# Real and imaginary halves of a spectrum stacked on the 128 partitions, in a kernel of two long convolutions mixed by a gate

## The chip, the cores and the metric

The kernel runs on one core of one Trainium2 chip. The metric is the device time of one execution in microseconds (us). The time of the kernel before is 413.97 us, the median of 3 runs (412.12 to 418.88).

## The reference, cut to what matters

Two sequences of 2048 positions with 448 channels are convolved along the positions, each with a kernel of its own per channel, and mixed by a gate. Both convolutions are written as products of spectra of padded length 4096.

```python
g = sigmoid((u * gate_w).sum(-1, keepdims=True))
# branch A: the kernel comes from 256 complex modes per channel
K  = einsum("dn,dnl,dn->dl", C, exp(dt * A * l), dt * B).real
a  = irfft(rfft(pad(u)) * rfft(pad(K)))[:2048] + u * Dskip
# branch B: the kernel ssm_k is an input; its signal is made from k and v
kv = shift_conv4(k, shift_k) * v
b  = u * (irfft(rfft(pad(kv)) * rfft(pad(ssm_k)))[:2048] + kv * ssm_D)
out = g * a + (1 - g) * b
```

## The kernel before, in words

**Layout.** A position is 64 a + b (a from 0 to 31, b from 0 to 63). A tile in natural order has 4 groups of channels times 32 values of a on its 128 partitions, and the 64 values of b times 112 channels along its free axis. The 112 channels are two halves h of 56, and these are worked on in four quarters H of 14 (`NW`), so one quarter holds 4 x 2 x 14 channels.

**One transform** of a quarter takes two steps. `spread` (L209) is the transform over a: for each of 14 channel columns one TensorE matmul takes the data (b and h, 128 columns) as weights and the table `W` (256 columns) as the moving operand. The result has b and h on the partitions, and 32 rows k, real and imaginary, along the free axis. ScalarE copies it from PSUM to the tile `zs` (L216, through `evac` at L534). `transform` (L219) is the transform over b, with the twiddle factors in its tables: for each of the 32 rows k it runs four matmuls of 56 columns (L229 to L232), cosine and sine against the real and the imaginary half, added up in PSUM. Each table is zero where h of the row and of the column differ, so half of the array multiplies by zero. ScalarE copies back to `zs` in pieces of 448 columns, two for every eight rows.

**Product and inverse.** `products` (L265) multiplies two spectra X and K in four VectorE products of 1792 columns, into T0 and in place. `stage_a` (L238) is the first step of the inverse: 14 columns with four matmuls of 256 columns each, 56 in all, added up in PSUM, copied to `U` by ScalarE. `stage_b` (L252) is the second step, 128 matmuls of 28 columns, and VectorE reads its PSUM in the epilogues (L682 for branch B, L688 and L691 for A).

**The kernel of branch A** is generated in eight blocks, two for a quarter (`KGen.block`, L294). VectorE builds powers by a doubling scheme (L311, L312, L316, L325, L332), 448 small matmuls with their weights (L345, `pk`) sum over the modes, a gather (L386, `ps_g`) rounds positions to their place, and the block's part of the quarter is spread (L674). Only then can the quarter's spectrum KA be transformed.

**Order.** `seq` (L747) is B0, B1, A0, B2, A1, B3, A2, A3. `step` (L705) does the inverse of one entry and the forward transforms of the next, and then one block of the kernel generator; behind it come block 7, the transform of KA for quarter 3 in four pieces whose PSUM copies are shared by ScalarE and VectorE (`evac_two`, L536), the products and the last inverse. Every engine works in its own order, which a scheduler writes from priorities when the program is built. Ahead of the loop lie the tables, the generator's setup (`kgen_setup`, L394, whose tables go out to DRAM and come back per block), the first two spectra of branch B, and the gate (L736 to L745: a product on VectorE, 112 matmuls, a sigmoid, two more VectorE passes).

**The kernel of branch B** is loaded by `load_sk` (L606) with eight DMAs that GpSimd issues. `sk_cols` (L613) has ScalarE reorder it into a second buffer `sk` (L616), and VectorE add the skip term to position 0 (L618). SBUF buffers come from rings: tag `q` (5 buffers of 7168 bytes per partition) and tag `hq` (7 of 3584 bytes). PSUM has three buffers of two banks for all matmuls but the generator's.

## Time and profile before

| what | value |
|---|---|
| time, median of 3 runs | 413.97 us |
| time of the profiled execution | 411.89 us |
| its span, first to last instruction | 409.7 us |
| mean granted TensorE clock | 0.845 |
| TensorE busy (matmuls) | 266.6 us, 65% |
| VectorE busy | 298.6 us, 73% |
| ScalarE busy | 225.8 us, 55% |
| GpSimd busy | 38.8 us, 9% |

The profile is one execution, recorded by the hardware. PE is TensorE's matmuls, PEld its weight loads, DVE is VectorE, ACT is ScalarE, POOL is GpSimd, SP is SyncE, which issues most DMAs. A row of the timeline has the start in us from the span's start, the duration, engine, line, operation, out<-in, shapes and a count; in brackets stands the idle time of the engine before it and what ended that. A group of instructions shows the total busy time and the mean duration in ns of one instruction. Durations of neighbours overlap a little, so the distance from start to start is the price of one in a row of many. A window lists the busy time of each engine in a stretch of the span, and the TensorE clock that was granted there, as a share of full speed.

### The profile page before, as it was taken

The numbers are of one execution on the slowest core, as the hardware profiler recorded it, in microseconds if no ns is written. First come the engines' busy times: TensorE is split into PE (matmuls) and PEld (weight loads), VectorE is DVE, ScalarE is ACT, GpSimd is POOL, SyncE is SP. The second block draws the span as 40 slices with busy tenths as digits, with TensorE's granted clock in tenths as the row PEclk, the third lists the DMA queues.
The fourth block names the chain that finished last, engine by engine and source line by source line (L and its number), as shares of the span: only waits on it lengthen the run. The fifth ranks groups of instructions, "written<-read, shape, count | busy, mean of one in ns | idle before, by whom it ended". The sixth has DMA issues, their size and how long they took to land.

```text
span 409.7 us, 13770 instructions
## 1 busy us (share of the span) xinstructions
PE 266.6 (65%) x6224; PEld 231.7 (57%) x6224; DVE 298.6 (73%) x525; ACT 225.8 (55%) x314; POOL 38.8 (9%) x166
## 2 busy tenths in 40 slices
PE   3001694250408997869777787896797997895770
PEld 2001531020408886767767675886597797695660
DVE  7969999755258598997999899899998820422630
ACT  6993948991630473555376266444782654656130
POOL 7940000000540000021000000000000000000000
PEclk9999966866665598996999896996999698898695
DMA  8979904799910012132120212121020000000019
GB/s 164 162 120 184 231 5 135 223 318 210 230 37 13 0 49 89 52 102 80 52 86 2 87 53 86 52 89 48 3 87 6 2 3 5 2 3 2 2 28 153
DMA packets 55826, 33.33 MB, mean 81 GB/s; under 512 B 37016, under 2 KB 53208, under 8 KB 55768
## 3 DMA queue, kind: packets, MB, share of 16 engines
q1 hardware_dynamic: 50200, 29.56, 31.3%
q0 software_dynamic: 1344, 1.98, 2.3%
q10 hardware_dynamic: 4224, 0.92, 1.4%
q8 instruction: 48, 0.79, 0.8%
q14 instruction: 10, 0.08, 0.1%
HBM read 19.84 MB, written 12.62 MB: 79 GB/s over the span
## 4 chain that ended last, share of the span: by engine, by line
PE 36%; DVE 31%; DMA 10%; issue 9%; ACT 8%; POOL 3%; DVEq 0%; ACTq 0%; POOLq 0%; SPq 0%
PE ps_a L247 10%; PE pk L345 7%; DVE kg_P L311 5%; PE ps_b L259 4%; DVE kvt L647 4%; ACT zsK L534 3%; PE ps_gate L739 3%; DMA skraw<-in_B_ssm_k_dram 3%; DMA ed<-ks_r 3%; PE ps_c L215 3%; PE ps L229 2%; DVE ks_ph L435 2%; PE ps L230 2%; PE ps L232 2%; PE ps L231 2%
## 5 line engine op out<-in xcount | busy, mean ns | idle before, releaser
L230 PEld LDWEIGHTS <-s_S 128*128 128x128 bf16 x512 | 52.8, 103 | 21.4 <-issue 21.4
L229 PE MATMUL ps<-zs,s_C 128*128 128x56 bf16 x384 | 46.6, 195 | 14.8 <-ACT zs L534 14.8
L229 PEld LDWEIGHTS <-s_C 128*128 128x128 bf16 x512 | 53.0, 103 | 0.3
L231 PEld LDWEIGHTS <-s_N 128*128 128x128 bf16 x512 | 52.8, 103 | 0.1
L232 PEld LDWEIGHTS <-s_C 128*128 128x128 bf16 x512 | 52.8, 103 | 0.0
L247 PE MATMUL ps_a<-sa_r,zs 128*128 128x256 bf16 x280 | 51.7, 292 | 0.7 <-DVE zs L274 0.4
L534 ACT CAST U<-ps_a 128x1024 bf16<-128x1024 f32 (+1 forms) x32 | 28.4, 908 | 37.0 <-PE ps_a L247 37.0
L534 ACT CAST zs<-ps 128x448 bf16<-128x448 f32 x96 | 43.4, 572 | 6.3 <-PE ps L232 6.3
L230 PE MATMUL ps<-zs,s_S 128*128 128x56 bf16 x384 | 46.6, 195 | 0.0
L231 PE MATMUL ps<-zs,s_N 128*128 128x56 bf16 x384 | 46.6, 195 | 0.0
L232 PE MATMUL ps<-zs,s_C 128*128 128x56 bf16 x384 | 46.5, 195 | 0.0
L311 DVE TENSOR_TENSOR kg_P<-kg_TQ,kg_EQ 128x896 bf16<-128x896 bf16 (+1 forms) x64 | 44.8, 711 | 1.6
L345 PE MATMUL pk<-kg_TP,kg_TQ 128*21 128x32 bf16 x1792 | 30.3, 238 | 21.5 <-issue 16.9
L534 ACT CAST zs<-ps_c 128x1024 bf16<-128x1024 f32 (+1 forms) x48 | 40.2, 957 | 5.6 <-PE ps_c L215 5.6
L345 PEld LDWEIGHTS <-kg_TQ 128*21 128x21 bf16 x1792 | 28.2, 121 | 24.1 <-issue 23.4
L247 PEld LDWEIGHTS <-zs 128*128 128x128 bf16 x280 | 35.6, 143 | 5.0 <-DVE zs L274 1.7
L247 PE MATMUL ps_a<-sa_r,T 128*128 128x256 bf16 x112 | 32.0, 289 | 6.1 <-ACT zs L534 3.1
L311 DVE TENSOR_TENSOR kg_P<-kg_TP,kg_EP 128x896 bf16<-128x896 bf16 (+2 forms) x24 | 29.9, 1246 | 0.7
L312 DVE TENSOR_TENSOR kg_TQ<-kg_P 128x224 bf16<-128x224 bf16 (+2 forms) x64 | 28.8, 450 | 2.1
L651 PE MATMUL ps_v<-kvt,ident 128*128 128x448 bf16 x64 | 19.8, 467 | 14.7 <-ACT kvt L534 7.9
L610 POOL DMA_DIRECT2D skraw<-in_B_ssm_k_dram x32 | 20.6, 651 | 72.5 <-ACT sk L616 68.5
L259 PE MATMUL ps_b<-U,sb_G 128*128 128x28 bf16 x1024 | 26.9, 174 | 0.7 <-ACT U L534 0.7
(162 smaller groups left out, 623.1 us busy)
## 6 DMA issues: line engine op xcount, KB each, us to landing
kg_EP<-ed SPq DMA_DIRECT2D x8, 840.0 KB, 4.2
ed<-ks_E SPq DMA_DIRECT2D x9, 672.0 KB, 4.0
kg_EQ<-ed SPq DMA_DIRECT2D x8, 476.0 KB, 3.4
ed<-ks_r SPq DMA_DIRECT2D x4, 896.0 KB, 9.8
kt<-in_B_k_dram SPq DMA_DIRECT2D x4, 448.0 KB, 9.7
skraw<-in_B_ssm_k_dram POOLq DMA_DIRECT2D x32, 56.0 KB, 3.8
vt<-in_B_v_dram SPq DMA_DIRECT2D x4, 448.0 KB, 8.3
uu<-in_A_u_dram SPq DMA_DIRECT2D x4, 448.0 KB, 11.2
```

The source lines that it names most:

```text
L229: nc.tensor.matmul(re, lhsT=c, rhs=zs[:, 0, k], start=True, stop=False)
L230: nc.tensor.matmul(re, lhsT=s, rhs=zs[:, 1, k], start=False, stop=True)
L231: nc.tensor.matmul(im, lhsT=m, rhs=zs[:, 0, k], start=True, stop=False)
L232: nc.tensor.matmul(im, lhsT=c, rhs=zs[:, 1, k], start=False, stop=True)
L247: nc.tensor.matmul(pt[:, i, :], lhsT=lhsT, rhs=r, start=(n == 0), stop=(n == 3))
L259: nc.tensor.matmul(o, lhsT=G[:, b, r].rearrange("p g a -> p (g a)"), rhs=U[:, r, b].rearrange("p w h -> p (w h)"), start=(r == 0), stop=(r ...
L311: V.tensor_tensor(out=P4[:, i * m:(i + 1) * m].rearrange("p n v c m -> p n v (c m)"), in0=in0, in1=in1, op=ALU.mult)
L312: V.tensor_tensor(out=T[:, dst:dst + n].rearrange("p n v m -> p (n v) m"), in0=P4[:, 0:n].rearrange("p n v c m -> p (n v) c m")[:, :, 0], ...
L345: nc.tensor.matmul(pt[32 * g:32 * g + NQ, hw, :].rearrange("p (i j) -> p i j", i=2), lhsT=TQ[:, :, c, m], rhs=rhs, start=(hf == 0 and c == 0),
L534: nc.scalar.copy(dst, src)
L610: nc.gpsimd.dma_start(raw[g * 32:(g + 1) * 32, :, h, :], sk_src[g, h][:, H * NW:(H + 1) * NW, :])
L651: nc.tensor.matmul(pt[:, i, 0:448], lhsT=ident[:], rhs=t[:, n, 4 * i:4 * i + 4, :].rearrange("p b l -> p (b l)"), start=(n == 0), stop=(n ...
```

## The change

**Stacked halves.** A `zs` tile now has real and imaginary on the two halves of the partitions (64 values of b each), and both halves h of the channels along the free axis: 32 rows k of 112 columns. `spread` does 28 columns with two matmuls each, real and imaginary, each with 64 weight columns and 128 moving columns, placed in the left or the right half of the array's columns (`tile_position`). The table `W2` holds for each row k the three blocks cosine, sine and cosine again, 64 columns each (with signs by partition), so that one full-array matmul of 112 columns transforms a row, and the same row shifted by one block gives the transform with real and imaginary halves exchanged.

**Swapped kernel spectrum.** For kernels (KB and KA) `transform` now makes both versions, `zs` and `zsS`; signals (XB and XA) have one. `products` is then two products of 3584 columns, and `stage_a` takes two matmuls of 128 columns per column of 28, 56 in all. PSUM copies of `transform` are 896 columns wide: four for a signal, eight for a kernel, where each had eight of 448.

**Beside these.** `sk_cols` leaves out ScalarE's reordering: the loaded tile is used as weights, and the skip term is added by GpSimd. The tables of the second step are written by ScalarE straight into place, without masks. The ring `q` has 6 buffers instead of 5, `hq` 6 instead of 7.

```diff
-NBQ = 5
-NBH = 7
+NBQ = 6
+NBH = 6
...
-def spread(nc, psum, W, zs, cols, w0, n, evac):
...
-            nc.tensor.matmul(pt[:, i, :], lhsT=cols(j + i), rhs=W[:], start=True, stop=True)
-        evac(zw[:, :, w0 + j:w0 + j + m, :], pt[:, 0:m].rearrange("p i (rk g) -> p rk i g", g=4))
+def spread(nc, psum, W, zs, cols, groups, evac):
+    for whs in groups:
+        pt = psum.tile([P, 8, 128], f32, name="ps_c", tag="ps")
+        for i, wh in enumerate(whs):
+            x = cols(wh)
+            for r in range(2):
+                nc.tensor.matmul(pt[64 * r:64 * r + 64, i, :], lhsT=x, rhs=W[:, 128 * r:128 * r + 128], start=True, stop=True,
+                                 tile_position=(0, 64 * r))
+        n = len(whs)
+        evac(zs[:].rearrange("p k (g c) -> p (k g) c", g=4)[:, :, whs[0]:whs[0] + n], pt[:, 0:n].rearrange("p i kg -> p kg i"))
...
-            nc.tensor.matmul(re, lhsT=c, rhs=zs[:, 0, k], start=True, stop=False)
-            nc.tensor.matmul(re, lhsT=s, rhs=zs[:, 1, k], start=False, stop=True)
-            nc.tensor.matmul(im, lhsT=m, rhs=zs[:, 0, k], start=True, stop=False)
-            nc.tensor.matmul(im, lhsT=c, rhs=zs[:, 1, k], start=False, stop=True)
-        for r in range(2):
-            evac(zs[:, r, 8 * kk:8 * kk + 8, :].rearrange("p k (g w) -> p k g w", g=4),
-                 pt[:, r, 0:8 * n].rearrange("p (k w g) -> p k g w", k=8, g=4), r)
+def transform(nc, psum, W, zs, evac, ks=range(4), swap=None):
+    n = 8 * NW
+    for kk in ks:
+        jobs = [(0, zs)] if swap is None else [(1, swap), (0, zs)]
+        done = []
+        for first, dst in jobs:
+            pt = psum.tile([P, 2, 512], f32, name="ps_2", tag="ps")
+            for i in range(8):
+                k = 8 * kk + i
+                nc.tensor.matmul(pt[:, i // 4, (i % 4) * n:(i % 4 + 1) * n],
+                                 lhsT=W[:, k, first:first + 2].rearrange("p r s -> p (r s)"), rhs=zs[:, k], start=True, stop=True)
+            done.append((dst, pt))
+        for i, (dst, pt) in enumerate(done):
+            evac(dst[:, 8 * kk:8 * kk + 8].rearrange("p (i k) c -> p i (k c)", i=2), pt[:, :, 0:4 * n], i)
...
+            for n, t in enumerate(terms):
+                nc.tensor.matmul(pt[:, i, :], lhsT=t[:].rearrange("p k (g c) -> p (k g) c", g=4)[:, :, j + i],
+                                 rhs=R[:, 128 * n:128 * n + 128], start=(n == 0), stop=(n == 1))
...
-    TT(out=fl(T0[:]), in0=x0, in1=y0, op=ALU.mult)
-    TT(out=x0, in0=x0, in1=y1, op=ALU.mult)
-    TT(out=y1, in0=x1, in1=y1, op=ALU.mult)
-    TT(out=x1, in0=x1, in1=y0, op=ALU.mult)
-    return T0[:], K[:, 1], X[:, 0], X[:, 1]
+def products(nc, X, K, S, k0=0, k1=32):
+    fl = lambda t: t[:, k0:k1].rearrange("p k c -> p (k c)")
+    for t in (K, S):
+        nc.vector.tensor_tensor(out=fl(t), in0=fl(t), in1=fl(X), op=ALU.mult)
+    return K, S
...
-        sk = hqt([P, NW, 64, 2], "sk")
-        nc.scalar.copy(sk[:].rearrange("p v b h -> p v h b"), raw[:])
-        s0 = sk[:, :, 0, :]
-        V.tensor_tensor(out=s0, in0=s0, in1=dB[:].rearrange("p (h v) -> p v h", h=2)[:, H * NW:(H + 1) * NW, :], op=ALU.add)
+        s0 = raw[:, :, :, 0]
+        nc.gpsimd.tensor_tensor(out=s0, in0=s0, in1=dB[:].rearrange("p (h v) -> p v h", h=2)[:, H * NW:(H + 1) * NW, :], op=ALU.add)
+        return lambda h, w: raw[:, w, h, :]
...
+    def with_swap(zs, ks=range(4), swap=None, ev=None):
+        swap = swap or qt([P, 32, 8 * NW], "zsS")
+        transform(nc, psum, W2, zs, ev or evac, ks, swap)
+        return zs, swap
```

Three places of the order are named in the prediction. The first is VectorE ahead of the gate, where the first signal of branch B has been transformed. L271 to L274 are the products (`T_1125` is T0), L618 adds the skip term to the kernel of quarter 1, L736 begins the gate. Before:

```order
L271 TENSOR_TENSOR T_1125<-zs 128x1792
L272 TENSOR_TENSOR zs<-zs 128x1792
L618 TENSOR_TENSOR sk<-sk,dB 128x14x2
L273 TENSOR_TENSOR zs<-zs 128x1792
L274 TENSOR_TENSOR zs<-zs 128x1792
L736 TENSOR_TENSOR ug<-uu,gw 128x7168
```

With the change (L255 is the product, L716 begins the gate):

```order
L146 TENSOR_SCALAR sb_G<-sb_v,mgB 128x32x32 x8
L255 TENSOR_TENSOR zs<-zs 128x3584
L255 TENSOR_TENSOR zsS<-zsS,zs 128x3584
L716 TENSOR_TENSOR ug<-uu,gw 128x7168
L297 COPY kg_TQ<-kg_EQ 128x224
```

The add has left VectorE, and nothing stands between the products and the gate.

The second is ScalarE in the setup. `ks_cs` are sines that the generator's tables wait for, `ps_c` and the numbered `ps_` tiles are PSUM of `spread` and `transform` for the first kernel of branch B. Before:

```order
L616 COPY sk<-skraw 128x14x2x64
L641 COPY wt<-wraw 128x448
L438 ACTIVATE ks_cs<-ks_ph 128x1792
L534 CAST zs<-ps_c 128x64x16 x3
L534 CAST zs<-ps_c 128x64x8
L438 ACTIVATE ks_cs<-ks_ph 128x1792 x3
```

With the change:

```order
L623 COPY wt<-wraw 128x448
L515 CAST zs<-ps_c 128x128x8 x3
L515 CAST zs<-ps_c 128x128x4
L515 CAST zsS<-ps_626 128x896
L515 CAST zs<-ps_635 128x896
L515 CAST zsS<-ps_646 128x896
L515 CAST zs<-ps_655 128x896
L515 CAST zsS<-ps_666 128x896
L419 ACTIVATE ks_cs<-ks_ph 128x1792
```

Nine PSUM copies now stand ahead of the first of these sines, and the reordering copy `sk` is gone.

The third is ScalarE at the kernel spectrum of quarter 2 of branch A (`zsK`). Before, its eight copies of 448 columns lay between two spreads:

```order
L534 CAST zsK<-ps_c 128x64x12
L534 CAST zsK<-ps_6333 128x448 x2
L534 CAST zsK<-ps_6368 128x448 x2
L534 CAST zsK<-ps_6403 128x448 x2
L534 CAST zsK<-ps_6438 128x448 x2
L534 CAST zs<-ps_c 128x64x16 x3
```

With the change there are eight copies of 896 columns:

```order
L515 CAST zsK<-ps_c 128x128x7 x2
L515 CAST zsS<-ps_5828 128x896
L515 CAST zsK<-ps_5837 128x896
L515 CAST zsS<-ps_5848 128x896
L515 CAST zsK<-ps_5857 128x896
L515 CAST zsS<-ps_5868 128x896
L515 CAST zsK<-ps_5877 128x896
L515 CAST zsS<-ps_5888 128x896
L515 CAST zsK<-ps_5897 128x896
L515 CAST zs<-ps_c 128x128x8 x3
```

The number of copies stays, their width doubles. On TensorE the last block's matmuls (`pk`) stand in the middle of this transform with the change, and ahead of the spread of `kg_KT` before.

More of the change, by code (lines that the diff above doesn't have):

```diff
@@ L128, in stage_a @@
         ph = self.tmp.tile([P, 4, 64], i32, name="sa_ph")
[L129 removed]
+        for i, off in enumerate((off_col[0][:, 0:1], off_col[1][:, 0:1], HALF, QUARTER)):
             self.phases(ph[:, i, :], j[:], s_col, off)
[L131 to L140 removed]
+        R = self.pool.tile([P, 256], bf16, name="sa_R")
+        nc.scalar.activation(R[:], low16(ph[:].rearrange("p i b -> p (i b)")), ACT.Sin, scale=PHASE)
+        return R
     def stage_b(self, pool, qt, hqt, k_col, mask):
@@ L206, in col_of @@
         return self.sel[:, self.var[key]].rearrange("p a b -> p (a b)")
-def spread(nc, psum, W, zs, cols, w0, n, evac):
-    zw = zs[:].rearrange("p r k (w g) -> p (r k) w g", g=4)
-    for j in range(0, n, 4):
-        m = min(4, n - j)
-        pt = psum.tile([P, 4, 256], f32, name="ps_c", tag="ps")
-        for i in range(m):
-            nc.tensor.matmul(pt[:, i, :], lhsT=cols(j + i), rhs=W[:], start=True, stop=True)
-        evac(zw[:, :, w0 + j:w0 + j + m, :], pt[:, 0:m].rearrange("p i (rk g) -> p rk i g", g=4))
@@ new lines, in stage_a @@
+def stage_a(nc, psum, pool, R, terms, evac):
+    U = pool.tile([P, 2, 64, 2 * NW], bf16, name="U", tag="q")
+    for j in range(0, 2 * NW, 8):
+        m = min(8, 2 * NW - j)
+        pt = psum.tile([P, 8, 128], f32, name="ps_a", tag="ps")
+        for i in range(m):
+            for n, t in enumerate(terms):
+                nc.tensor.matmul(pt[:, i, :], lhsT=t[:].rearrange("p k (g c) -> p (k g) c", g=4)[:, :, j + i],
+                                 rhs=R[:, 128 * n:128 * n + 128], start=(n == 0), stop=(n == 1))
+        evac(U[:, :, :, j:j + m].rearrange("p r b c -> p (r b) c"), pt[:, 0:m].rearrange("p i rb -> p rb i"))
```

127 lines of the change are left out of this document (40 added, 87 removed).

## The prediction

> **What bounds the kernel now.** I read the page's shares first, then windows of the engines, then what VectorE waited for behind the gate, then the timelines at the gate and at the end.
>
> ```profile
> PE 266.6 (65%) x6224; PEld 231.7 (57%) x6224; DVE 298.6 (73%) x525; ACT 225.8 (55%) x314; POOL 38.8 (9%) x166
> ```
>
> ```profile
> 124.00:142.40 18.40, 18.11 (x134) 16.73 (x135) 12.03 (x21) 3.83 (x6) 0.00 (x0) 0.50 0.01 3
> 142.40:318.70 176.30, 140.65 (x4179) 129.76 (x4178) 161.96 (x250) 96.15 (x154) 5.01 (x8) 0.92 0.18 59
> 318.70:400.00 81.30, 66.06 (x1518) 59.44 (x1517) 30.41 (x53) 40.51 (x64) 0.00 (x0) 0.86 0.04 7
> ```
>
> The columns are length, then PE, PEld, DVE, ACT and POOL busy, then TensorE's granted clock. No engine bounds the whole. From 142 to 319 us VectorE is busy 92% of the time and paces the loop, with TensorE at 80% close behind. Behind 319 VectorE has little left and TensorE is busy 81%.
>
> ```profile
> DVE ept L688 <- PE ps_b L259: 21.6, 2, 12.0
> DVE T L271 <- ACT zsK L534: 12.2, 1, 12.2
> DVE ug L682 <- PE ps_b L259: 8.5, 3, 7.6
> DVE kg_TP L325 <- PE pk L345: 8.2, 5, 2.3
> ```
>
> These are VectorE's longest waits from 140 us on. The first three lie in the tail. In the loop it waits mainly for `pk`: 8.2 us, five times.
>
> ```profile
> 325.17 2.02 DVE L332 TENSOR_TENSOR kg_TP<-kg_TP,kg_EP 128x3584 bf16<-128x3584 bf16 x1
> 338.29 1.85 PE L345 MATMUL pk<-kg_TP,kg_TQ 128*21 128x32 bf16 x110 [0.62 <-ACT kg_S L534]
> 340.72 1.96 PE L345 MATMUL pk<-kg_TP,kg_TQ 128*21 128x32 bf16 x114 [0.58 <-issue]
> 349.73 1.09 DVE L271 TENSOR_TENSOR T<-zs,zsK 128x1792 bf16<-128x1792 bf16 x1 [12.17 <-ACT zsK L534]
> 360.58 1.50 ACT L534 CAST U<-ps_a 128x1024 bf16<-128x1024 f32 x2 [0.41 <-PE ps_a L247]
> 377.94 0.53 ACT L538 CAST zsK<-ps 128x448 bf16<-128x448 f32 x1 [1.79 <-PE ps L232]
> 385.71 0.39 DVE L274 TENSOR_TENSOR zs<-zs,zsK 128x448 bf16<-128x448 bf16 x1
> 392.35 1.50 ACT L534 CAST U<-ps_a 128x1024 bf16<-128x1024 f32 x2 [0.62 <-PE ps_a L247]
> ```
>
> VectorE finishes its part of the last block at 327.2, and TensorE takes that block's `pk` up only at 338.3: it is 11.1 us behind. I therefore split the time into what lies ahead of the gate, the loop up to 327.2, and the 82.5 us from there to the end at 409.7.
>
> **Prices.**
>
> ```profile
> 362.34 3.59 ACT L534 CAST zs<-ps 128x448 bf16<-128x448 f32 x8 [0.25 <-PE ps L232]
> 138.80 6.57 ACT L534 CAST zs<-ps_c 128x1024 bf16<-128x1024 f32 x8 [0.63 <-PE ps_c L215]
> L311 DVE TENSOR_TENSOR kg_P<-kg_TP,kg_EP 128x3584 bf16<-128x3584 bf16 x8 | 16.2, 2023 | 0.2
> L312 DVE TENSOR_TENSOR kg_TP<-kg_P 128x1792 bf16<-128x1792 bf16 x8 | 8.7, 1087 | 0.1
> L616 ACT COPY sk<-skraw 128x1792 bf16<-128x1792 bf16 x4 | 9.1, 2276 | 3.9 <-DMA skraw<-in_B_ssm_k_dram 3.9
> 258.37:264.64 6.27, 6.27 (x64) 1.00 0.11 22
> 264.48:267.95 3.47, 3.47 (x137) 1.00 0.33 117
> L247 PEld LDWEIGHTS <-zs 128*128 128x128 bf16 x280 | 35.6, 143 | 5.0 <-DVE zs L274 1.7 <-issue 0.8 <-DVE kg_P L311 0.7
> 310.77 0.77 PE L386 MATMUL ps_g<-kg_S,ga_sel 128*32 128x112 bf16 x52
> ```
>
> The two windows are one `stage_a` and one `transform` on TensorE alone. `stage_a` streams 56 x 256 columns in 6.27 us, 2.29 columns per ns. With half the columns it takes 3.1 us if weight loads stay hidden, and 56 x 0.143 = 8.0 if each load shows in full. In `transform` a load and its matmul come every 26 ns (3.47 us over 137), so loads do overlap; I take 3.3, a saving of 3.0. A signal's `transform` streams 3584 columns, 1.6 us instead of 3.5; a kernel's two streams take 3.1.
>
> A ScalarE cast of 448 columns costs 3.59/8 = 0.45 us from start to start. The eight of the spread are six of 1024 and two of 512 (the row names the first shape only), so a column costs 0.8 ns and a cast of 896 is 0.81. A signal then holds ScalarE 3.2 us instead of 3.6, a kernel 6.5, which is 2.9 more. The copy `sk` (2.28) goes. The spreads cast as many columns as before, and their writes in runs of 8 elements instead of 16 I cost at nothing, since `U` was already written in runs of 8.
>
> A product of 3584 columns costs 2.02, so a pair 4.05 instead of four times 1.09: 0.3 less.
>
> The new `spread` has no row: 64 weight columns, 128 moving ones, half of the array. The gather shows four matmuls in four parts of the array: 52 start within 0.77 us. About 37 of a block's 58 have 112 columns, some 4100 columns in 1.06 us, 1.7 times `stage_a`'s rate, so parts of the array do work at once. At that rate 56 x 128 columns take 1.8 us; one after the other, 56 ns each, 3.1. Both hide behind the 3.3 us in which ScalarE empties a spread. If a load of 143 ns shows each time it is 8.0, which is a rival below. I take nothing.
>
> **Ahead of the gate.**
>
> ```profile
> 103.60 2.40 ACT L534 CAST zs<-ps_c 128x1024 bf16<-128x1024 f32 x3
> 109.16 2.71 ACT L534 CAST zs<-ps 128x448 bf16<-128x448 f32 x6 [0.41 <-PE ps L232]
> 112.67 1.09 DVE L272 TENSOR_TENSOR zs<-zs 128x1792 bf16<-128x1792 bf16 x1
> 115.74 2.18 ACT L616 COPY sk<-skraw 128x1792 bf16<-128x1792 bf16 x1 [3.87 <-DMA skraw<-in_B_ssm_k_dram]
> 117.95 0.19 DVE L618 TENSOR_TENSOR sk<-sk,dB 128x28 bf16<-128x28 bf16 x1 [4.19 <-ACT sk L616]
> 120.26 3.88 DVE L736 TENSOR_TENSOR ug<-uu,gw 128x7168 bf16<-128x7168 bf16 x1
> 37.57 1.70 ACT L438 ACTIVATE ks_cs<-ks_ph 128x1792 bf16<-128x1792 int16 x1 [6.17 <-DVE ks_ph L435]
> 24.20 4.05 DMA skraw<-in_B_ssm_k_dram
> 37.73 1.27 DVE L137 TENSOR_SCALAR sa_r<-sa_v,mhA 128x128 bf16<-128x128 bf16 x6
> L451 DVE TENSOR_TENSOR ks_E<-ks_cs,ks_mag 128x1792 bf16<-128x1792 bf16 x9 | 9.8, 1083 | 3.7 <-ACT ks_cs L438 3.7
> ```
>
> VectorE's add for a later quarter stands between the products and waits for a DMA and a copy, so two products and the gate come 4.19 us late. With the add on GpSimd, the casts of the spread end near 106.4, four casts behind a cold TensorE near 110.3, two products at 114.4, the gate's product at 118.3 instead of 124.1: -6.0. GpSimd then waits for the DMAs instead; behind it stand only later loads of the same kind, wanted much later. The ring `hq` loses a buffer, but also `sk` and T0; `sb_j` and `sb_v` then share two, which moves the last phases behind eight `sb_G` and is in the 106.4.
>
> Against this, nine casts now stand ahead of the sine at 37.57, for which VectorE's setup waits. The data land at 28.3; the first PSUM tile is there some 2 us later, and the casts take 3.3 + 5 x 0.81 = 7.3. That ends at 37.6, no loss, if TensorE keeps up, and near 40.4, 2.8 late, if it is paced by PSUM buffers that the transposes still hold. I take +1.5. The masks that VectorE no longer applies to the tables gain nothing: it waits for ScalarE right behind the first (3.7 us before `ks_E`), and the second (1.27) filled the wait for the sine at 37.57; the bound is those 1.27. The sum for this part is **-4.5**.
>
> **The loop, up to 327.2.** VectorE stays the pace. Five pairs of products save 1.4 and three adds 0.3. The 8.2 us behind `pk` come from holes in its issue that the change does not touch:
>
> ```profile
> 314.28 2.09 PE L345 MATMUL pk<-kg_TP,kg_TQ 128*21 128x32 bf16 x128 [0.62 <-issue]
> 318.28 0.35 PE L345 MATMUL pk<-kg_TP,kg_TQ 128*21 128x32 bf16 x10 [1.91 <-issue]
> ```
>
> Between none and all of them can go; I take 1.5. So -3.2 (bounds -1.7 and -9.9), and VectorE ends its last block at 327.2 - 4.5 - 3.2 = 319.5. TensorE must be there too: six `stage_a` (18.0) and six signals (11) save 29 us against the 11.1 it was behind. ScalarE gives back 5.5 kernels x 2.9 = 16 and takes 9 off, and was idle 80 of 176 us.
>
> **The tail, from there to the end.** `pk` starts at once: 6.4 with its holes (312.2 to 318.6), then half of the kernel's transform, which now lies behind it, 3.7: products at +10.1, where before they came at +22.5. Products and `stage_a` with its last cast: 4.1 + 4.6 = 8.7, before 12.4. The last signal, `stage_b` and the gather chain to KA's transform: 13.4, before 14.1, of which the last 8.3 stay. The shared transform: VectorE per quarter a cast of 896 (0.62 for 448 before; bounds 0.62 and 1.24, taken 1.1) and two products of about 0.55, 8.6 in all and 1.5 ahead of it, 10.1, before 9.9. The last `stage_a`: 5.6 with TensorE cold at its start, before 7.8. `stage_b`, epilogue, stores: 15.8 as before. Sum 63.7 instead of 82.5: **-18.8**.
>
> Together 319.5 + 63.7 = 383.2 of span, -26.5. The profiled execution has 411.9 with 409.7 of span, so the forecast is 383.2 + 2.2 = 385.4, taken as **386 us**; the profiled execution is 2 below the median of the runs, within their spread.
>
> **The rivals.**
>
> *ScalarE becomes the pace.* A kernel's casts take 6.5 us on a path that ScalarE works in order, between the gather and the next spread; then TensorE is as late for the last `pk` as now, and 11.1 of the tail's gain is lost: 386 + 11 = 397. For it: casts were already slower than `transform`'s matmuls (3.59 against 3.47). Against it: 45% idle in the loop.
> The Trainium skill, "TensorEngine Tiling (Array Packing)", section PSUM Bottleneck, says that after such a gain on TensorE the copies out of PSUM may become the bottleneck. The trace agrees for the single transform, by the two numbers above.
>
> *The waits of VectorE vanish too*: all 8.2 behind `pk` instead of 1.5, 386 - 7 = 379. Against it: the issue holes.
>
> *TensorE turns cold and nothing is gained.* In the window from 124 it was 98% busy and had half the clock, so being busy did not keep it fast. With 141 - 29 = 112 us of work at a clock of 0.92 the loop is TensorE's from a clock of 0.59 down; at 0.5 it takes 206 us, 30 more than 176, of which the gain eats nearly all: about 411, no change. Against it: 0.92 in the loop.
>
> *The half-array spread shows its loads: slower.* 14 spreads lie behind the gate. With one load of 143 ns for each of 56 matmuls a spread takes 8.0 us, 4.7 above ScalarE's 3.3: 66 us, less some 16 that the loop hides: 386 + 50 = 436. It turns slower than now from 6.3 us a spread, 112 ns a matmul. Against it: the gather's 15 ns.
> The same page, under Gotcha 2: Feature Incompatibilities, says that column tiling excludes fast weight load, and the page "TensorE: Matmul & The Clock Gate", section LDWEIGHTS, prices a plain load at its columns over 1.2 per ns; an estimate by it is 53 ns for 64 columns, 3.0 us a spread, which would leave the sum as it is. No row here has such a load.
>
> **How the numbers follow.** Forecast 0.60 (its own range 378 to 394, from the bounds of the setup, the waits and the tail), ScalarE 0.18, no waits 0.07, cold 0.07, slower 0.08. The range from 374 to 403 holds the first three. A measurement of this kernel tells about 2%, 8 us, from no change, so faster is 0.85, same 0.07, slower 0.08.
>
> **What would show it.** Right: `ug` of the gate starts near 116 and no VectorE wait stands between the products; the last `kg_TP` ends near 320 and `pk` follows within 1 us; `stage_a` lasts near 3.3 us on a warm clock; casts of 896 come every 0.8 us; spreads stay at ScalarE's 3.3. Wrong: `pk` of the last block late by over 5 us (ScalarE), a mean clock under 0.7 (cold), over 60 ns a matmul in the spreads (loads), or waits of VectorE in the loop above 15 us.

## The result and the profile after

The changed kernel takes 394.95 us, the median of 4 runs (394.0 to 397.07), where the kernel before took 416.12 on the same chip (4 runs, 412.12 to 418.88). The ratio is 0.953, with a 95% interval from 0.942 to 0.963: faster. On the four other chips used below the kernel before has medians of 412.43 to 413.65 (7 to 19 runs each), so 416.12 is on the high side; against those the gain is 17 to 19 us rather than 21. The forecast of 386 us was 9 too low: inside the range from 374 to 403, which was drawn to hold two rivals as well, but just outside the forecast's own range from 378 to 394. The profiled execution took 395.71 us with a span of 393.9, so against the profile of before (span 409.7) 15.8 us are gone; the forecast was 26.5.

From the page of the changed kernel, the busy shares of the engines and the shares of the chain that ended last; behind it the chain's line from the page of the kernel before.

```profile
PE 250.7 (64%) x5616; PEld 222.4 (56%) x5616; DVE 292.3 (74%) x494; ACT 239.4 (61%) x278; POOL 39.2 (10%) x168
...
PE 30%; ACT 27%; DVE 26%; issue 7%; DMA 6%; POOL 1%; ACTq 0%; DVEq 0%; SPq 0%
```

```profile
PE 36%; DVE 31%; DMA 10%; issue 9%; ACT 8%; POOL 3%; DVEq 0%; ACTq 0%; POOLq 0%; SPq 0%
```

ScalarE's share of the chain went from 8% to 27%, about 33 to 106 us, although its busy time grew by 13.6 us only. It did not become the busiest engine; it came in between, tile by tile, behind TensorE.

The stretches that the prediction used, from the start of the gate's matmuls to VectorE's last block and from there to the end. The columns are length, PE, PEld, DVE, ACT and POOL busy, then TensorE's clock; the kernel after first, then the one before.

```profile
120.80:327.05 206.25, 168.43 (x4328) 156.70 (x4329) 182.83 (x268) 125.58 (x157) 5.66 (x10) 0.86 0.17 51
327.05:393.90 66.85, 41.42 (x971) 39.29 (x968) 20.48 (x31) 30.11 (x37) 0.00 (x0) 0.76 0.17 30
```

```profile
124.29:327.19 202.90, 167.24 (x4365) 153.53 (x4366) 181.94 (x275) 105.95 (x166) 5.01 (x8) 0.87 0.16 52
327.19:409.70 82.51, 57.57 (x1466) 52.37 (x1464) 22.23 (x45) 34.54 (x57) 0.00 (x0) 0.83 0.14 25
```

The gate's matmuls start 3.5 us earlier, the loop behind them is 3.35 us longer, and the tail is 15.7 us shorter. So the whole gain shows behind VectorE's last block, where TensorE and not VectorE had the work.

The waits of VectorE from 139 us on, and the timeline of the tail:

```profile
DVE ept L671 <- PE ps_b L247: 17.1, 2, 8.8
DVE zsS L255 <- ACT zsS L515: 12.1, 3, 9.8
DVE zsK L521 <- PE ps L220: 8.7, 1, 8.7
DVE kg_TP L306 <- PE pk L326: 5.3, 4, 1.6
DVE ug L665 <- PE ps_b L247: 4.2, 4, 1.8
```

```profile
116.78 3.97 DVE L716 TENSOR_TENSOR ug<-uu,gw 128x7168 bf16<-128x7168 bf16 x1
...
318.52 1.16 DVE L665 TENSOR_TENSOR ug<-ps_b,ug 128x448 bf16<-128x448 f32 x2 [1.19 <-PE ps_b L247]
...
325.03 2.02 DVE L313 TENSOR_TENSOR kg_TP<-kg_TP,kg_EP 128x3584 bf16<-128x3584 bf16 x1
329.07 2.46 PE L326 MATMUL pk<-kg_TP,kg_TQ 128*21 128x32 bf16 x150
336.88 2.03 DVE L255 TENSOR_TENSOR zsS<-zsS,zs 128x3584 bf16<-128x3584 bf16 x1 [9.82 <-ACT zsS L515]
342.17 3.53 ACT L515 CAST U<-ps_a 128x1024 bf16<-128x1024 f32 x4 [1.27 <-PE ps_a L234]
353.22 1.86 PE L205 MATMUL ps_c<-WcK,kg_KT 128*64 128x128 bf16 x28 [1.50 <-ACT kg_KT L515]
357.23 1.86 PE L205 MATMUL ps_c<-WcK,kg_KT 128*64 128x128 bf16 x28 [1.15 <-ACT kg_KT L515]
360.46 4.64 PE L220 MATMUL ps<-zsK,s_W 128*128 128x112 bf16 x48 [1.38 <-ACT zsK L515]
370.64 0.33 PE L234 MATMUL ps_a<-sa_R,zsK 128*128 128x128 bf16 x1 [4.00 <-DVE zsK L255]
```

VectorE ends its last block (`kg_TP`, L313) at 327.05, and TensorE takes `pk` up 2.0 us later, where it was 11.1 before. The products for quarter 2 follow 9.8 us after `kg_TP`, not 22.5.

Last, what TensorE is busy with in the stretch from the gate's product on VectorE to the end of the span, as windows of one source line each: `stage_a` (L234), `spread` (L205), `transform` (L220), with length, PE busy, count and clock; the last row is the window of all lines, with all engines. After:

```profile
116.78:393.90 277.12, 33.69 (x448) 0.83 0.17 46
116.78:393.90 277.12, 48.81 (x784) 0.83 0.17 46
116.78:393.90 277.12, 49.89 (x672) 0.83 0.17 46
116.78:393.90 277.12, 209.86 (x5296) 195.99 (x5296) 207.33 (x300) 155.69 (x193) 9.68 (x17) 0.83 0.17 46
```

And before, L247, L215, L229 and all lines (the four lines of `transform` alternate, and each gives a row like that of L229):

```profile
120.26:409.70 289.44, 58.34 (x448) 0.85 0.16 45
120.26:409.70 289.44, 34.86 (x196) 0.85 0.16 45
120.26:409.70 289.44, 55.19 (x448) 0.85 0.16 45
120.26:409.70 289.44, 224.82 (x5828) 205.93 (x5828) 208.21 (x322) 140.49 (x223) 7.97 (x13) 0.85 0.16 45
```

`stage_a` gave 24.6 us and `transform` 5.3, but `spread` took 13.9 back. That makes 16.0; the other lines took 1.0 more, so 15.0 us of TensorE's time are gone, and the stretch is 12.3 us shorter. VectorE's busy time there is the same within 1 us.

### The profile page after: what moved, and what is told of

It is laid out like the page before. It is cut to its first block, busy times and chain, and to the rows that moved or that the text cites. A ratio compares the mean times of both kernels' runs of the same rounds, so it can differ in the third digit from the quotient of the medians.

```text
span 393.9 us, 12469 instructions
## 1 busy us (share of the span) xinstructions
PE 250.7 (64%) x5616; PEld 222.4 (56%) x5616; DVE 292.3 (74%) x494; ACT 239.4 (61%) x278; POOL 39.2 (10%) x168
## 4 chain that ended last, share of the span: by engine, by line
PE 30%; ACT 27%; DVE 26%; issue 7%; DMA 6%; POOL 1%; ACTq 0%; DVEq 0%; SPq 0%
PE pk L326 7%; PE ps_c L205 6%; ACT zs L515 6%; PE ps_b L247 6%; ACT zsK L515 5%; ACT U L515 4%; DVE kg_P L292 4%; PE ps_a L234 4%; DVE kvt L629 4%; PE ps_gate L719 3%; ACT zsS L515 3%; DMA ed<-ks_r 3%; PE ps L220 2%; DVE zsS L255 2%; ACT ks_mag L400 2%
## 5 line engine op out<-in xcount | busy, mean ns | idle before, releaser
L220 PEld LDWEIGHTS <-s_W 128*128 128x128 bf16 x768 | 51.4, 113 | 24.7 <-issue 23.6
L220 PE MATMUL ps<-zs,s_W 128*128 128x112 bf16 x512 | 36.6, 224 | 12.3 <-ACT zs L515 8.0
L515 ACT CAST zs<-ps 128x896 bf16<-128x896 f32 x48 | 41.9, 959 | 1.0 <-PE ps L220 1.0
L326 PE MATMUL pk<-kg_TP,kg_TQ 128*21 128x32 bf16 x1792 | 29.9, 238 | 12.4 <-issue 12.3
L633 PE MATMUL ps_v<-kvt,ident 128*128 128x448 bf16 x64 | 19.3, 454 | 27.9 <-DVE kvt L629 20.0
L515 ACT CAST zsS<-ps 128x896 bf16<-128x896 f32 x28 | 26.3, 939 | 12.5 <-PE ps L220 12.5
L234 PE MATMUL ps_a<-sa_R,zsS 128*128 128x128 bf16 x224 | 32.6, 241 | 1.0 <-issue 1.0
L292 DVE TENSOR_TENSOR kg_P<-kg_TP,kg_EP 128x896 bf16<-128x896 bf16 (+2 forms) x24 | 29.9, 1247 | 0.8
L234 PEld LDWEIGHTS <-zsS 128*128 128x128 bf16 x224 | 30.2, 153 | 0.1
L247 PEld LDWEIGHTS <-sb_G 128*128 128x128 bf16 x1024 | 27.4, 97 | 4.2 <-issue 4.0
L247 PE MATMUL ps_b<-U,sb_G 128*128 128x28 bf16 x1024 | 27.7, 176 | 3.0 <-ACT zs L515 1.8
L220 PE MATMUL ps<-zsK,s_W 128*128 128x112 bf16 x256 | 21.8, 270 | 6.3 <-ACT zsK L515 5.5
L255 DVE TENSOR_TENSOR zsS<-zsS,zs 128x3584 bf16<-128x3584 bf16 (+1 forms) x11 | 16.6, 1511 | 12.1 <-ACT zsS L515 12.1
L205 PE MATMUL ps_c<-Wc,kv 128*64 128x128 bf16 x224 | 15.0, 302 | 15.3 <-ACT zs L515 11.9
L205 PEld LDWEIGHTS <-kv 128*64 128x64 bf16 x224 | 14.9, 220 | 16.3 <-issue 12.0
## 6 DMA issues: line engine op xcount, KB each, us to landing
uu<-in_A_u_dram SPq DMA_DIRECT2D x4, 448.0 KB, 11.1
```

What stands on the lines that cost most here:

```text
L205: nc.tensor.matmul(pt[64 * r:64 * r + 64, i, :], lhsT=x, rhs=W[:, 128 * r:128 * r + 128], start=True, stop=True, tile_position=(0, 64 * r))
L220: nc.tensor.matmul(pt[:, i // 4, (i % 4) * n:(i % 4 + 1) * n], lhsT=W[:, k, first:first + 2].rearrange("p r s -> p (r s)"), rhs=zs[:, k], ...
L234: nc.tensor.matmul(pt[:, i, :], lhsT=t[:].rearrange("p k (g c) -> p (k g) c", g=4)[:, :, j + i], rhs=R[:, 128 * n:128 * n + 128], start=(n ...
L247: nc.tensor.matmul(o, lhsT=G[:, b, r].rearrange("p g a -> p (g a)"), rhs=U[:, r, b], start=(r == 0), stop=(r == 1))
L255: nc.vector.tensor_tensor(out=fl(t), in0=fl(t), in1=fl(X), op=ALU.mult)
L292: V.tensor_tensor(out=P4[:, i * m:(i + 1) * m].rearrange("p n v c m -> p n v (c m)"), in0=in0, in1=in1, op=ALU.mult)
```

## The experiments

Each kernel is compared with the kernel before on its own chip. "Stretch" is the time from the start of the gate's product on VectorE to the end of the profiled span, and the busy times are those in it. Both are of one execution, which lies up to 3.7 us from its kernel's median (e2 3.7 and e9 1.9 below it, e5 2.9 and e1 2.3 above; the profile of before 2.1 below the 413.97 of its first three runs), so a difference of 2 or 3 us in these columns tells nothing by itself.

| kernel | median us | ratio to before (95%) | stretch | TensorE | VectorE | ScalarE |
|---|---|---|---|---|---|---|
| before | 416.12 | | 289.4 | 224.8 | 208.2 | 140.5 |
| changed | 394.95 | 0.953 (0.942 to 0.963) | 277.1 | 209.9 | 207.3 | 155.7 |
| e1 | 411.54 | 0.996 (0.992 to 0.999) | 293.2 | 223.9 | 208.3 | 143.6 |
| e2 | 416.24 | 1.006 (1.002 to 1.010) | 294.9 | 232.6 | 208.8 | 156.1 |
| e3 | 382.27 | 0.926 (0.920 to 0.932) | 258.4 | 194.6 | 203.1 | 136.2 |
| e4 | 395.13 | 0.956 (0.950 to 0.962) | 278.5 | 211.7 | 207.3 | 155.8 |
| e5 | 396.44 | 0.961 (0.956 to 0.966) | 277.1 | 209.9 | 203.6 | 137.1 |
| e6 | 394.09 | 0.954 (0.949 to 0.959) | 275.1 | 198.3 | 207.9 | 155.3 |
| e7 | 393.45 | 0.953 (0.948 to 0.958) | 274.5 | 207.5 | 197.7 | 155.2 |
| e8 | 387.39 | 0.939 (0.934 to 0.943) | 268.9 | 196.9 | 207.5 | 153.6 |
| e9 | 388.97 | 0.941 (0.935 to 0.947) | 270.0 | 196.4 | 208.0 | 132.8 |
| e10 | 418.02 | 1.011 (1.005 to 1.017) | 299.9 | 237.8 | 207.6 | 156.4 |
| e11 | 393.21 | 0.951 (0.945 to 0.956) | 275.4 | 209.5 | 207.8 | 156.1 |
| e12 | 389.84 | 0.944 (0.940 to 0.949) | 276.6 | 210.0 | 221.9 | 144.9 |

The theory at first was that of the prediction: VectorE paces the loop, and TensorE's saved time counts in the tail alone. The rivals: TensorE's time counts everywhere; ScalarE's doubled casts do.

**e1, one part alone: the skip term on GpSimd, in the kernel before.**

```diff
-        V.tensor_tensor(out=s0, in0=s0, in1=dB...
+        nc.gpsimd.tensor_tensor(out=s0, in0=s0, in1=dB...
```

> The kernel before with one part of the change alone: GpSimd instead of VectorE adds the skip term of branch B's kernel. Theory (the add held VectorE up ahead of the gate, and what is won there carries to the end): no VectorE wait of 4.19 us stands between the products, the gate's product starts at 120.3 - 4.2 = about 116 us, the last kg_TP ends near 323 and the run is about 4 us shorter, a ratio near 0.990. Rival (TensorE, 11 us behind at the end of the loop, sets the end and takes the gain back): the gate starts 4 us earlier, but the time moves by less than 1.5 us.

The gate's product starts at 118.89, only 1.4 us earlier, and the time is 0.4% less (2.1 us by the medians). Both theories had the gate start 4 us earlier, so the run does not decide between them. The wait of 4.19 us is gone, but what it had held back came forward:

```profile
39.26 0.97 ACT L534 CAST zs<-ps 128x448 bf16<-128x448 f32 x2 [0.47 <-PE ps L232]
40.11 1.71 ACT L438 ACTIVATE ks_cs<-ks_ph 128x1792 bf16<-128x1792 int16 x1
```

With the add off VectorE the first kernel's spread and casts start 8 us earlier and stand ahead of the sine `ks_cs`, which begins at 40.11 where it began at 37.57. The first product ahead of the gate then starts 2.8 us later (114.30 against 111.47). A gain of 4.2 came out as 1.4.

**e4, the same delay undone in the changed kernel.** The casts of the first kernel transform are ordered behind that sine:

```diff
+    def evac_late(dst, src, i=0):
+        after(tc, nc.scalar.copy(dst, src), p0_sine)
-    KB[0] = with_swap(spread_in(sk_cols(0)))
+    KB[0] = with_swap(spread_in(sk_cols(0)), ev=evac_late)
```

> The changed kernel with one order set by hand: on ScalarE the eight casts of the first kernel spectrum stand behind the sine that VectorE's setup waits for, instead of five of them ahead of it. Theory (the casts ahead of the sine made the setup 2.2 us later, and this carries through to the gate): the sine starts near 38 us instead of 39.8, the tables' stage starts 1.5 to 2.2 us earlier, the gate's product starts near 115 instead of 116.8, the time is about 2 us shorter. Rival (the delay is swallowed by later waits, of the stores of the tables for one): the gate moves by less than 0.5 us.

The sine starts at 37.53 (39.76 in the changed kernel) and the gate's product at 114.50 instead of 116.78, as the theory said. Of these 2.3 us, 0.9 are left at the end of the profiled span, and the medians (395.13 and 394.95) show none. So the delay carries to the gate, but its worth at the end is below what these runs can tell.

**e2 and e10, TensorE's saving given back.** Every matmul of `stage_a` is done twice, in e2 with a free order, in e10 with the order of the three engines held at that of the changed kernel (`keep_order` chains the instructions of an engine in a list's order, without a wait). The edit of e10:

```diff
-            for n, t in enumerate(terms):
+            for n, t in list(enumerate(terms)) * 2:
...
+    keep_order(tc, nc)
```

> The changed kernel with every matmul of stage_a done twice, so that the first inverse step costs TensorE about 7.5 us again instead of 3.8 (6.3 in the kernel before), and nothing else changes. Theory (in the loop VectorE is the pace and TensorE's saved time is worth nothing there; it counts in the tail alone): the last kg_TP ends within 3 us of 327.1, the two inverses of the tail pay 3.8 and about 4.5, the time grows by 8 to 10 us, a ratio near 0.975 to the kernel before. Rival (what TensorE saves is what moves the whole kernel): eight inverses by 3.8 us, +25 to +30 us, slower than the kernel before.

> The changed kernel with every matmul of stage_a done twice, as before, but with the order on the three engines held at that of the changed kernel. Theory A (the chain through the end runs over TensorE and ScalarE in turn, and each of the eight inverses stands in it): 3.8 us each, 25 to 30 us in all, 420 us or more. Theory B (VectorE paces the loop and TensorE's time counts in the tail alone): 8 to 10 us, about 404. The free order gave 416.

Neither size was met in e2: by its median it is 21 us above the changed kernel, not 9 and not 25. There the last `kg_TP` ended at 323.1, earlier than in the changed kernel, and the whole cost lay behind it, in a tail of 87.7 us; the scheduler had put branch B's last epilogue behind `kg_TP` again. That was the first sign that the end of VectorE's last block decides nothing. In e10, with the same order, all stages are longer. Its whole stretch, its loop and its tail:

```profile
116.67:416.60 299.93, 237.75 (x5744) 224.96 (x5744) 207.64 (x300) 156.40 (x193) 9.64 (x17) 0.85 0.16 43
120.66:341.93 221.27, 187.78 (x4666) 177.03 (x4667) 183.17 (x268) 126.11 (x157) 5.65 (x10) 0.89 0.16 48
341.93:416.60 74.67, 49.97 (x1082) 47.92 (x1079) 20.48 (x31) 30.28 (x37) 0.00 (x0) 0.77 0.15 26
```

27.9 us more of TensorE's time make the stretch 22.8 us longer; in e2 it is 17.8 for 22.8. Each us added to TensorE costs about 0.8 us by these executions, 0.8 to 0.9 by the medians (23.1 us in e10, 21.3 in e2). In e10 it costs that in the loop (15.0 us for 19.4) as well as in the tail (7.8 for 8.6). The theory that TensorE's time counts in the tail alone is refuted, the first rival is nearly right.

**e7, VectorE's work taken away.** The second product is left out for the five pairs between gate and loop end:

```diff
-    for t in (K, S):
+    for t in (K, S) if both else (K,):
```

> The changed kernel with the second product left out for the five pairs that VectorE multiplies between gate and the end of the loop (so those cross products are not the reference's): VectorE has 5 x 2.02 = 10.1 us less to do there, the other engines the same. Theory A (VectorE alone still paces the loop): the time falls by 8 to 10 us, to about 386. Theory B (after the change TensorE and ScalarE, taking turns tile by tile, are as late as VectorE, and the loop has no single pace): it falls by less than 5 us, and VectorE waits longer for ps_b and the casts instead.

VectorE is 9.6 us less busy, its last `kg_TP` ends at 313.1, 14 us earlier (2.3 of them because the four L665 stand behind it again), and the stretch is 2.6 us shorter, the median 1.5 (the ratio is the changed kernel's). That is theory B. It waits instead, for the same casts as before:

```profile
311.06 2.03 DVE L313 TENSOR_TENSOR kg_TP<-kg_TP,kg_EP 128x3584 bf16<-128x3584 bf16 x1
...
333.63 2.03 DVE L255 TENSOR_TENSOR zsS<-zsS,zs 128x3584 bf16<-128x3584 bf16 x1 [16.58 <-ACT zsS L515]
```

The wait of 9.82 us became 16.58. VectorE, the busiest engine of the loop, is not its pace in the changed kernel.

**e8, TensorE's work taken away.** One of the two terms of `stage_a` is left out.

```diff
-            for n, t in enumerate(terms):
-                nc.tensor.matmul(pt[:, i, :], ... start=(n == 0), stop=(n == 1))
+            n, t = i % 2, terms[i % 2]
+            nc.tensor.matmul(pt[:, i, :], ... start=True, stop=True)
```

> The changed kernel with one matmul instead of two for each column of stage_a (left out: one of the two terms of each inverse), so TensorE works 1.9 us less in each of the eight inverses. Theory A (TensorE's time counts in the tail alone): 1.9 and about 3 us there, 4 to 5 us in all, 390 to 391 us. Theory B (ScalarE's casts of U, 0.9 us each, follow TensorE tile by tile, so that stage_a cannot get shorter than about 3.5 us with its last cast): 1 to 3 us in all. Rival C (TensorE sets the whole chain): 12 us or more.

TensorE is 12.9 us less busy, the stretch 8.2 us shorter, the median 7.6: more than the tail alone could give, less than the full sum. None of the three theories has the size.

**e3, e5, e6 and e9, the swapped spectra.** Left out are the matmuls and the casts (e3), the casts alone (e5), the matmuls alone (e6), and both again with the order held (e9; there VectorE keeps its four casts of the last kernel, which in e3 ScalarE does).

The edit of e3:

```diff
-        jobs = [(0, zs)] if swap is None else [(1, swap), (0, zs)]
+        jobs = [(0, zs)]
...
-    for t in (K, S):
-        nc.vector.tensor_tensor(out=fl(t), in0=fl(t), in1=fl(X), op=ALU.mult)
+    for t in (S, K):
+        nc.vector.tensor_tensor(out=fl(t), in0=fl(K), in1=fl(X), op=ALU.mult)
```

e5 has the same products, and e6 those of the changed kernel; their edits in `transform`, e5's first:

```diff
         for i, (dst, pt) in enumerate(done):
+            if dst is zs:
-            evac(dst[:, 8 * kk:8 * kk + 8]...
+                evac(dst[:, 8 * kk:8 * kk + 8]...
```

```diff
-        jobs = [(0, zs)] if swap is None else [(1, swap), (0, zs)]
+        jobs = [(0, zs)]
...
-            done.append((dst, pt))
+            done += [(dst, pt)] if swap is None else [(swap, pt), (dst, pt)]
```

e9 is e3's edit with `keep_order`.

> The changed kernel without the swapped kernel spectra: a kernel is transformed once, four casts instead of eight, and the second product takes the plain spectrum again, so VectorE's products cost the same (left out: the swapped spectra, so the cross products are not the reference's). Theory (ScalarE's doubled casts cost only where they stand on the chain: in the setup, in the last two kernels): the gate 1 to 2 us earlier, the loop between gate and last kg_TP within 3 us of 206.3, the tail 7 us shorter (3.2 for the kernel of quarter 2, about 4 for the shared transform), together -8 to -11 us, about 385 us. Rival (ScalarE paces the loop and keeps VectorE waiting there): the loop alone is 6 us or more shorter, -15 us or more in all.

> The changed kernel with the swapped spectra's matmuls kept and their casts out of PSUM left out (so the second product takes the plain spectrum, and the cross products are not the reference's). It splits the 12.9 us that the kernel without swapped spectra won. Theory (it is ScalarE's second four casts, 3.3 us a kernel, that stand in the chain): 381 to 386 us, nearly all of the gain. Rival (it is the second eight matmuls for every eight rows, 1.6 us a kernel on TensorE): 391 us or more.

> The counterpart: the swapped spectra's matmuls left out and all casts kept, each PSUM tile of a kernel's transform cast twice, into both spectra (left out: the transform with exchanged halves). Theory (ScalarE's casts): 391 to 396 us, no more than 4 below the changed kernel's 395. Rival (TensorE's matmuls): 387 us or less.

> The changed kernel without the swapped spectra's matmuls and casts, as in the kernel of that name, but with the order of the instructions on TensorE, VectorE and ScalarE held at that of the changed kernel, so that only the work is gone and the scheduler cannot write another order (left out: the swapped spectra). Leaving out the casts alone or the matmuls alone had won nothing, both together 13 us. Theory A (the order that the scheduler wrote for that kernel won the 13 us): 389 us or more, so less than 6 us for the work. Theory B (both were on the chain, one behind the other, so that either alone hides behind the other): 381 to 386 us here too.

e3 won 12.7 us by its median, but in an order that cannot be set beside that of the changed kernel: its gate's product starts at 120.42, 3.6 us later and not earlier, and its last `kg_TP` ends at 335.5. Either half alone won nothing that the medians show (396.44 and 394.09): 18.6 us less of ScalarE (e5) left the stretch at 277.1, 11.6 us less of TensorE (e6) took 2.0 off. For e5 this is not sharp, because its gate too starts 3.6 us later and its profiled execution lies 2.9 us above its median; behind the gate it may have won 2 or 3 us. With the order held, both together are worth 7.1 us of stretch, and 6.0 by the medians. e9's window of all engines, and the chain's line of its page:

```profile
115.31:385.30 269.99, 196.35 (x5072) 184.72 (x5072) 207.96 (x300) 132.84 (x165) 12.71 (x17) 0.80 0.17 47
```

```profile
DVE 44%; PE 24%; ACT 10%; issue 8%; DMA 7%; POOL 4%; DVEq 0%; ACTq 0%; POOLq 0%; SPq 0%
```

There ScalarE is back at 10% of the chain, and VectorE has 44% of it. So in this order VectorE's own chain seems to lie only some 7 us below that of TensorE and ScalarE: with the swapped spectra the latter decides, without them VectorE. The shares of the chain are all that this rests on. The median of 388.97 is at the edge of theory A and outside theory B: about half of e3's gain is the work. The rest came with e3's other order and the four casts that VectorE no longer does (4.4 us busy); its stretch is 11.6 us shorter than e9's, its gate 5.1 us later. How the casts and the matmuls share the 7 us stays open, since e5 and e6 each ran in an order of their own.

**e11, the order alone.** All work of the changed kernel, TensorE in e3's order:

```diff
+    keep_order(tc, nc)
```

> The changed kernel with all of its work, but TensorE in the order that the scheduler wrote for the kernel without swapped spectra (the swapped matmuls put right ahead of the plain ones of the same rows); VectorE and ScalarE ordered by the scheduler around it. Theory A (the order alone is worth several us): the time differs from 395 by 4 us or more. Theory B (work and dependencies set the time, the order matters little): 392 to 398 us.

393.21 us, as theory B said: TensorE's order alone is worth nothing that can be told here.

**e12, a version from what the runs point to.** Branch B's first signal is written ahead of the tables of `stage_b`, and in the tail VectorE takes every other cast.

```diff
+    def evac_alt(dst, src, i=0):
+        turn[0] ^= 1
+        evac_two(dst, src, turn[0])
...
-    G = cons.stage_b(kgp, qt, hqt, k_col, mask_b)
+    XB[0] = spread_in(lambda h, w: kvq[0][:, :, h, w])
+    transform(nc, psum, W2, XB[0], evac)
+    terms = {("B", 0): products(nc, XB[0], *KB[0])}
+    G = cons.stage_b(kgp, qt, hqt, k_col, mask_b)
...
-            U = stage_a(nc, psum, qp, R, terms[c], evac)
+            U = stage_a(nc, psum, qp, R, terms[c], evac_alt if j == 6 else evac)
```

> The changed kernel, all of its work, with two things that the runs point to. First, branch B's first signal (spread, transform, products) is written ahead of the tables of the second inverse step, so that its casts and products do not wait behind them (VectorE waited 4.9 us for these casts, and 6.3 us ahead of the tables). Second, from the kernel of quarter 2 on, where VectorE waits 9.8, 8.3 and 8.8 us in the tail, VectorE takes every other cast out of PSUM (the transforms, U, the last gathers and spreads). Theory (at the end the chain runs through ScalarE's casts, and VectorE's waits there are free time): the gate starts 4 to 7 us earlier, the tail is 3 to 5 us shorter, 384 to 389 us. Rival (VectorE's casts take 1.09 us where ScalarE's follow each other by 0.81, and stand behind the generator's last products in VectorE's order, so that sharing wins nothing): the gain is the gate's alone or less, 390 us or more.

389.84 us, 5.6% below the kernel before; its six runs (388.6 to 391.2) all lie below the changed kernel's four, on another chip, while the intervals of the two ratios overlap. The gate's product starts at 111.94, 4.8 us earlier. The stretch behind it is 276.6, the changed kernel's within 0.6: 10.8 us moved from ScalarE to VectorE won nothing there, and TensorE's busy time is the same. The rival was right, its bound of 390 us missed by 0.2.

## Why the prediction was right and where it failed

The span came out 10.7 us longer than forecast (393.9 for 383.2): 1.0 of it lies ahead of the gate, 6.6 in the loop and 3.1 in the tail.

**Faster, by the mechanism in the tail: right.** TensorE is no longer behind at the end of the loop: `pk` of the last block follows 2.0 us after `kg_TP`, where it was 11.1 (foretold at once, within 1). `stage_a` takes 3.77 us on a warm clock (foretold 3.3), casts of 896 follow each other by 0.80 us (0.81), the products come 9.8 us behind `kg_TP` (10.1), products and `stage_a` with the last cast take 8.8 (8.7), the shared transform 10.2 (10.1). That the 9.8 is so near is partly luck: `pk` began 2.0 us late, and from there to the products it took 2.3 us less than the sum had.

**Ahead of the gate: 3.5 instead of 4.5 us.** The step that was short is the price of the casts ahead of the sine: 2.2 us, where +1.5 was taken. The rest came out at -5.7 for -6.0. e1 shows the pieces: 4.2 won, 2.8 lost, of which 2.5 stand at the sine behind the casts that move up.

**The loop: the step that failed.** It was "VectorE stays the pace", worth -3.2; the loop became 3.35 us longer. In VectorE's own time: products and adds 1.7 less; the last epilogue of branch B, four L665 (2.3 us), now stands ahead of the last `kg_TP` in its order, where it stood behind it; the waits for `pk` fell by 2.9 (8.2 to 5.3; 1.5 was taken), but waits for `ps_b` rose from 0.5 to 4.2 and those for the casts of a product's input from 0.5 to 2.3. -1.7 + 2.3 - 2.9 + 3.7 + 1.8 = +3.2. And it hardly matters when VectorE ends there: e7 moved that end by 14 us and the median by 1.5.

**What set the end instead** is, as far as the runs show, TensorE with ScalarE behind each of its tiles: giving TensorE 27.9 us of work back in the same order (e10) takes the whole gain away and 1% more. At the 0.8 that e2 and e10 show, the 15.0 us saved would be 12.0 of the 12.3 by which the stretch shrank. This is an estimate: the price comes from work added, work taken away won less (8.2 for 12.9 in e8, 2.0 for 11.6 in e6), and no run lightens TensorE in the kernel before. That VectorE is not far behind, as e9's chain suggests, would explain the difference.

**The spread "at nothing": mis-sized.** It takes 48.8 us of TensorE behind the gate instead of 34.9, 784 matmuls of 62 ns busy time. The prediction had 1.8 to 3.1 us a spread and hid it behind ScalarE's 3.3; it is 3.5 on the average (48.81/14), and the two half spreads of the tail take 1.86 where 0.97 stood:

```profile
370.42 0.97 PE L215 MATMUL ps_c<-WcK,kg_KT 128*128 128x256 bf16 x7 [1.50 <-ACT kg_KT L534]
```

Not every spread became dearer. These are two of the changed kernel, of the loaded kernel `skraw` and of the signal `kv`, by the same line with the same table; below them the weight loads of the two tiles, count and min/median/max in ns first.

```profile
196.75 0.64 PE L205 MATMUL ps_c<-Wc,skraw 128*64 128x128 bf16 x16 [0.26 <-ACT zsK L515]
200.20 3.72 PE L205 MATMUL ps_c<-Wc,kv 128*64 128x128 bf16 x56 [0.50 <-ACT zs L515]
...
L205 PEld LDWEIGHTS <-skraw x224: 106/118/178, 29.0 to 269.5; 128*64 128x64 bf16 x112
L205 PEld LDWEIGHTS <-kv x224: 195/222/222, 91.2 to 273.6; 128*64 128x64 bf16 x112
```

From start to start a matmul takes 28 ns with `skraw` and some 60 with `kv`. The 64 weight columns of `skraw` lie next to each other in SBUF (`raw[:, w, h, :]`), those of `kv`, `uu` and `kg_KT` 28, 112 and 14 elements apart (for `kv`: `kvq[H][:, :, h, w]`). Behind the gate the spreads of these three tiles together went from 28.2 to 41.6 us of TensorE, the fourth from 7.2 to 7.9. In the kernel before, the gaps did not show: with `uu` and with `sk` a matmul of 256 columns came every 109 ns. So the prediction's bounds held for adjacent columns (2.6 us a spread, 7.9/3) and not for the others (3.8, 41.6/11). That the layout is the cause is read from these four tiles; no run changed it for one of them.

`transform` was mis-sized too: the 32 matmuls of a signal follow each other by 49 ns, 1.6 us in one row as foretold, but they come in four groups of eight, and each group takes 0.55 us to the end of its last matmul, 2.2 in all. Together with `stage_a` (-24.6, as foretold: 8 x 3.0) the forecast's prices add up to some -40 us of TensorE (24 + 7 signals x 1.9 + 7 kernels x 0.4), and 16.0 came from these three. The Trainium skill, "TensorEngine Tiling (Array Packing)", section Gotcha 2: Feature Incompatibilities, says that column tiling gives up fast weight load. The slow loads of `kv`, `uu` and `kg_KT` agree with it; the 28 ns of `skraw`, column-tiled as well, show that this alone does not make a spread slow.

**The tail: 66.85 instead of 63.7.** The mis-sized terms: the way from the last cast of `U` to the last transform is 14.8 us instead of 13.4, mostly by the two half spreads; the last `stage_a` with its casts 6.9 instead of 5.6, since TensorE had waited 4.0 us and ran it at a clock of 0.53; the end 16.4 instead of 15.8.

**The rivals.** *ScalarE becomes the pace* came half true: its share of the chain tripled, but `pk` was 2.0 us late and not over 5, the sign named for it, e5 took 18.6 us off ScalarE and won little or nothing, and e12 took 10.8. Its forecast of 397 is nearest to the measured time, for a reason that only partly is its own. The Trainium skill, "TensorEngine Tiling (Array Packing)", section PSUM Bottleneck, says that after a fourfold speedup of TensorE the copies out of PSUM may become the bottleneck. The chain agrees so far as they came onto the path at a far smaller speedup (27% against 8%, with TensorE's 224.8 us down to 209.9); in e5 and e12 taking copies off ScalarE alone did not help. *Cold* did not come (a clock of 0.80, before 0.845), nor did *all waits vanish*. The half-array spread did show over 60 ns a matmul, the sign named for it (62 busy, 59 from start to start in an unbroken row of `uu`), but far from the break-even of 112.

## What to carry to other kernels

The busiest engine need not be the pace: take work off it, or add some to another, and see whether the end moves. Here 10 us less of VectorE (89% busy in that loop) gave 2, and each us more of TensorE cost 0.8 to 0.9. When a change trades one matmul form for another, add up the busy time of all of TensorE's lines: the step taken "at nothing" ate nearly half of what the others won (13.9 of 29.9 us). Look there at how the weight columns of the new form lie in SBUF: in this kernel the half-array matmul was cheap where they were adjacent and twice as dear where they were not. And a wait that is removed lets what stood behind it move up, here in front of a sine that the setup needed.

## What the runs showed of the hardware

Matmuls with a load each kept pace with their moving columns, at a granted clock of 1.00 and in an unbroken row. From start to start one of 56 columns took 26 ns (`transform` before), one of 112 columns 49 (`transform` now), one of 128 columns 63 (`stage_a` now), one of 256 columns 109 (`stage_a` before). A group takes longer, by the time from the start of its last matmul to that one's end: 0.2 us, which made eight of 112 columns 0.55 us instead of 0.39. Halving the columns of `stage_a` saved 40% (3.77 us for 6.27).

Two column halves of the array worked at once where the 64 weight columns were adjacent: with `skraw`, 16 matmuls of 128 moving columns, alternating left and right, took 0.64 us, 28 ns each from start to start, less than half of the 63 of `stage_a` and well under the 49 of 112 columns. With weight columns 14 to 112 elements apart the two matmuls of a pair still started within 21 ns of each other, but the next pair came some 120 ns after the last, and 28 took 1.86 us: no gain over full-array matmuls.

The clock showed in two windows of the changed kernel, over `stage_a` of quarter 2 and the last `stage_a`:

```profile
340.90:344.67 3.77, 3.77 (x60) 3.77 (x61) 0.00 (x0) 2.50 (x3) 0.00 (x0) 1.00 0.00 0
370.64:376.68 6.04, 6.04 (x56) 5.92 (x57) 0.00 (x0) 2.69 (x3) 0.00 (x0) 0.53 0.01 3
```

The same 56 matmuls took 3.77 us at a granted clock of 1.00 and 6.04 at 0.53, after an idle time of 4.0 us (the first window also counts a few records of its neighbours).
